# Retention before two MLPs: token tiles of 128 become tiles of 64, worked in the four quarters of the TensorE array

## The chip, the core and the metric

The kernel runs on one core of a Trainium2 chip. The metric is device time in microseconds (us): the median of three runs, and beside it one profiled execution from which all rows here come. The engines of the core are TensorE (PE for its matmuls, PEld for its weight loads), VectorE (DVE), ScalarE (ACT), GpSimd (POOL) and SyncE (SP), which issues most of the transfers.

## What is computed

```python
# q, k, v: (4 batches, 8 heads, 576 tokens, 64)
scores = q @ k.T / 8
D[i, j] = gamma[h] ** (i - j) if i >= j else 0
x = (scores * D) @ v                      # (4*576 tokens, 8*64 features)
x = softplus(x @ w1_in) @ w1_out          # 512 -> 2048 -> 512
out = h * sigmoid(1.702 * h) @ w2_out     # h = x @ w2_in
```

The retention can be written with a running state per head: for tokens in tiles, the output is the masked product inside the tile plus the query times the state of all earlier tiles, and the state is decayed and added to by k.T @ v of each tile.

## The kernel before, in words

**Stages.** All matmuls of the MLPs are done with numbers split in a high and a low part (three products of 128x128 weights with 512 tokens each). First comes the retention of batch 0 alone (`first_batch`, L402 on), while the weights of the first MLP arrive as 64-bit words. Then `run_mlps` (L134) walks over work items: for each block of tokens (batches 0, 1, 2, then the tails of all batches, then batch 3) and each of 16 slices f of the hidden size, `mm1` makes 12 matmuls into a PSUM bank `ph`, `start` and `split` apply the activation (ACT, L188) and split it (ACT L77, DVE L82: `gh` and `gl`), and `mm2` of two items earlier makes 12 more. The second MLP repeats this from 489 us on.

**What is woven in.** `side()` is called four times per item. It advances two generators. One is `batch(b + 1)`: while the first MLP works on batch b, the retention of the next batch is emitted in steps (rate 0.52 per call; three calls of the generator per step: scale, matmuls, the rest). The other is `convert` (L85): it turns the 64-bit words of a weight slice into high and low halves with ACT (L94, L77) and DVE (L106, L107, L111, L82). During batch 0's items it makes the first MLP's weights, one slice `w` per item, and item f cannot start before slice f is made. From batch 1's items on it makes the second MLP's weights, half a slice at a time, read from and written back to DRAM by SP (L498, L509), through two buffers.

All engines work through their instructions in the order in which they were emitted, so one that waits holds up what stands behind it.

**The retention step** (`step`, L287) handles for two heads and a chunk of 256 tokens (c is 0 or 1) the output of an earlier chunk, `out_i`, and the scores and states of a new one, `i`. A chunk is two tiles of 128 tokens. Each batch has 8 chunks and 9 steps; a chunk with c = 1 also takes the 64 tokens at the end of the sequence (`e`).

- Matmuls, all plain float32 (each product shows as two MATMUL rows): state times query and value times masked scores go to `po` by `put` (L297), 128 rows deep, with the two heads in the two column halves of the array; so do the new states. The scores `k` by `q` (L326) are 64 rows deep with the two heads in the two row halves and in two banks, `ps`.
- DVE: four state updates of 64x64 (L338, L79), the masked and decayed scores `a` of 128x256 for each head (L351), those of the last 64 tokens (L355), and the output, `po` times the decay of the query, to `xf` (L361) and `xt` (L366). For the batches 0 and 1 (`on_act`) the second head's `a` is made by ACT (L345) and POOL (L347).
- ACT also scales the keys in `scale_pair` (L285).

In `first_batch` the output of a chunk comes two steps after its scores, the banks alternate between two sets, and FILL = 2 matmuls on a constant tile (`warm`, L441) follow each step.

Of the kernel before, what the change touches and what calls it, by code (L numbers as in the profile page):

```python
# [18 lines left out]
ENDS = 320  # L19
# [3 lines left out]
FILL = 2  # L23
# [4 lines left out]
def kernel(  # L28
# [193 lines left out]
    with tc.manual_schedule():  # L222
# [28 lines left out]
        with first:  # L251
# [4 lines left out]
            mask = ac.tile([P, 5, D], F32, name="mask")  # L256
            dec = ac.tile([P, 2 * H + 2 * NPAIR], F32, name="dec")
            odec = ac.tile([P, NPAIR, P], F32, name="odec")
            rdec, sdec = dec[:, 0:H], dec[:, H:2 * H]
            r2dec, gdec = dec[:, 2 * H:2 * H + NPAIR], dec[:, 2 * H + NPAIR:]  # L260
            svs = [[ac.tile([P, P], F32, name=f"sv{i}_{j}") for j in range(4)] for i in range(2)]
# [19 lines left out]
            def scale_pair(i):  # L281
                p, x = pairs[i][2], loaded[i][2]
                for h in range(2):
                    y = x[:, :, halves[h]]
                    nc.scalar.mul(y, y, sdec[:, 2 * p + h:2 * p + h + 1])  # L285

            def step(out_i, i, banks, on_act, later):  # L287

                po, ps = banks[0], banks[1:]
                ends_at = slice(2 * C0 - D, 2 * C0)
                cols = [slice(C0 + (t + 1) * D, C0 + (t + 2) * D) for t in range(2)]
                clear = [True, True]

                def put(h, at, l, rhs):
                    nc.tensor.matmul(po[halves[h], at], l, rhs, start=clear[h], stop=True, skip_group_check=True)  # L297
                    clear[h] = False

                if out_i is not None:  # L300
                    b, c, p = pairs[out_i]
                    _, q, _, v, e = loaded.pop(out_i)
                    a = masked.pop(out_i)
                    states = [None] + svs[p % 2] if c == 0 else svs[p % 2][1:]
                    for t in range(2 + c):
                        j = slice(t * P, t * P + (P if t < 2 else D))
                        if states[t] is not None:
                            for h, r in enumerate(halves):
                                put(h, j, states[t][:, r], q[:, j] if t < 2 else e[:, P:P + D])
                        for h, r in enumerate(halves):  # L310
                            if t < 2:
                                put(h, j, v[:, t, r], a[:, h * C0 + t * P:h * C0 + (t + 1) * P])
                            else:
                                put(h, j, e[:, P + D + h * D:P + D + (h + 1) * D], a[:, 2 * C0:])
                if i is not None:
                    b, c, p = pairs[i]
                    k, q, x, v, e = loaded[i]
                    if c:
                        for h, r in enumerate(halves):
                            put(h, ends_at, e[:, r], e[:, P:P + D])  # L320
                    for t in range(2):
                        for h, r in enumerate(halves):
                            put(h, cols[t], x[:, t, r], v[:, t, r])
                    for j in (slice(0, P), slice(P, C0)):
                        for h, r in enumerate(halves):
                            nc.tensor.matmul(ps[h][:, j], k[r, j], q[r, j], start=True, stop=True)  # L326
                if later:
                    yield
                if i is not None:
                    b, c, p = pairs[i]  # L330
                    states = [None] + svs[p % 2] if c == 0 else svs[p % 2][1:]
                    for t in range(2):
                        for r in halves:
                            sv, new = states[t + 1][r, r], po[r, cols[t]]
                            if states[t] is None:
                                hi("v", sv, new)
                            else:
                                nc.vector.scalar_tensor_tensor(  # L338
                                    out=sv, in0=states[t][r, r], scalar=gdec[r, p:p + 1], in1=new,
                                    op0=ALU.mult, op1=ALU.add)  # L340
                    a = ap.tile([P, 2 * C0 + D], F32, tag="a", name="a", bufs=2)
                    for h in range(2):
                        ah, rd = a[:, h * C0:(h + 1) * C0], rdec[:, 2 * p + h:2 * p + h + 1]
                        if h and on_act:
                            nc.scalar.mul(ah, ps[h][:, 0:C0], rd)  # L345
                            ah = ah.rearrange("p (t j) -> p t j", t=2)
                            nc.gpsimd.affine_select(  # L347
                                out=ah, in_=ah, compare_op=ALU.is_ge, fill=0.0,
                                base=0, pattern=[[0, 2], [1, P]], channel_multiplier=-1)
                            continue  # L350
                        nc.vector.scalar_tensor_tensor(  # L351
                            out=ah, in0=ps[h][:, 0:C0], scalar=rd,
                            in1=mask[:, 0:4, :].rearrange("p t j -> p (t j)"), op0=ALU.mult, op1=ALU.mult)
                    if c:
                        nc.vector.scalar_tensor_tensor(  # L355
                            out=a[:, 2 * C0:], in0=po[:, ends_at], scalar=r2dec[:, p:p + 1],
                            in1=mask[:, 4, :], op0=ALU.mult, op1=ALU.mult)
                    masked[i] = a
                if out_i is not None:
                    b, c, p = pairs[out_i]  # L360
                    nc.vector.tensor_tensor(  # L361
                        out=xf[b][:, p, c * C0:(c + 1) * C0].rearrange("p (t j) -> p t j", t=2),
                        in0=po[:, 0:C0].rearrange("p (t j) -> p t j", t=2),
                        in1=odec[:, p:p + 1, :].to_broadcast([P, 2, P]), op=ALU.mult)
                    if c:
                        nc.vector.tensor_tensor(  # L366
                            out=xt[:, p, b * TAIL:(b + 1) * TAIL], in0=po[:, C0:C0 + D], in1=odec[:, p, 0:TAIL],
                            op=ALU.mult)
# [4 lines left out]
            def batch(b):  # L373

                xf[b] = xf_tile()
                i0, i1 = 2 * NPAIR * b, 2 * NPAIR * (b + 1)
                for i in range(i0, i0 + RB):
                    load_pair(i)
                yield
                for i in range(i0, i1 + 1):  # L380
                    if i < i1:
                        scale_pair(i)
                    yield
                    out_i = i - 1 if i > i0 else None
                    banks = [bank(ps_h, "h"), bank(ps_a, "s"), bank(ps_a, "o")]
                    yield from step(out_i, i if i < i1 else None, banks, b < 2, True)
                    if out_i is not None and out_i + RB < i1:
                        load_pair(out_i + RB)
                    yield

            def first_batch():
# [24 lines left out]
                for i in range(n + 2):  # L416
# [5 lines left out]
                    for _ in step(i - 2 if i >= 2 else None, i if i < n else None, banks, True, False):  # L422
                        pass
# [21 lines left out]
            for sv in svs[0] + svs[1]:  # L445
                nc.vector.memset(sv, 0.0)
            nc.vector.memset(mask, 1.0)
            nc.gpsimd.affine_select(
                out=mask[:, 0:4, :].rearrange("p (t u) j -> p t (u j)", u=2),
                in_=mask[:, 0:4, :].rearrange("p (t u) j -> p t (u j)", u=2), compare_op=ALU.is_ge, fill=0.0,  # L450
                base=0, pattern=[[0, 2], [1, P]], channel_multiplier=-1)
            for h, r in enumerate(halves):
                nc.vector.tensor_copy(mask[r, 4, :], mask[r, h, :])
# [133 lines left out]
def _decays(H):  # L587
    import numpy as np

    gamma = (1.0 - 2.0 ** (-5.0 - np.arange(H, dtype=np.float32))).astype(np.float64)  # L590
    p = np.arange(P)
    pair = np.repeat(gamma.reshape(H // 2, 2), 64, axis=1).T
    d = [gamma ** -p[:, None], gamma ** (P - p[:, None]), pair ** -(p[:, None] % 64), pair ** P]
    o = gamma[:, None] ** p[None, :] / 8.0
    o = np.repeat(o.reshape(H // 2, 2, 1, P), 64, axis=2).reshape(H // 2, P, P).transpose(1, 0, 2)
    return [np.ascontiguousarray(a.astype(np.float32)) for a in (np.concatenate(d, axis=1), o)]
# [50 lines left out]
```

## Time and profile before

| | |
|---|---|
| median of 3 runs | 893.33 us (892.29 to 894.74) |
| profiled execution | 891.51 us |
| its span on the core | 889.8 us |
| PE busy | 874.7 us, 98% |
| PEld busy | 722.7 us, 81% |
| DVE busy | 401.6 us, 45% |
| ACT busy | 309.4 us, 35% |
| POOL busy | 28.1 us, 3% |

Busy time is a sum over stages that differ: the retention and the conversion of weights fill the first 350 us, and the rest is matmuls of the MLPs. The ends of matmuls are modelled, so that a PE shown as busy may still wait a little. The chain of waits follows the work that ended last back in time and tells what each piece waited for.

### The profile page before, as it was taken

How to read it: one execution, taken by the hardware profiler on the slowest of the kernel's cores; microseconds unless marked ns; L12 is line 12 of the kernel's file. 1: busy time of each engine (PE TensorE's matmuls, PEld its weight loads, DVE VectorE, ACT ScalarE, POOL GpSimd, SP SyncE). 2: the span in 40 equal slices, each digit the busy share in tenths (PEclk: the TensorE clock that was granted, in tenths of full speed). 3: DMA queues.
4: the chain of work that ended last, by engine and by line, in shares of the span. 5: the costliest groups of instructions: out<-in, count | busy, mean ns of one | idle time of the engine just before them, and what ended most of it. 6: DMA issues, size and time to landing. Idle time of an engine off the chain costs nothing.

```text
span 889.8 us, 12120 instructions
## 1 busy us (share of the span) xinstructions
PE 874.7 (98%) x4928; PEld 722.7 (81%) x4928; DVE 401.6 (45%) x743; ACT 309.4 (35%) x557; POOL 28.1 (3%) x57
## 2 busy tenths in 40 slices
PE   9799999999989999999999999999999999999997
PEld 5488888888868888998888888888888888988886
DVE  6998973777567765112112322332233223333222
ACT  4556544444444434323223222232222223232221
POOL 1000001000000000001000100000000000000000
PEclk9999999999999999999999999999999999999999
DMA  9925531565576653103555600020002000201001
GB/s 353 382 80 202 203 115 48 207 215 200 189 260 224 242 198 143 49 1 119 191 192 193 228 1 1 0 95 1 1 1 71 1 1 13 84 1 24 0 1 48
DMA packets 33784, 101.73 MB, mean 114 GB/s; under 512 B 3392, under 2 KB 5440, under 8 KB 31680
## 3 DMA queue, kind: packets, MB, share of 16 engines
q1 hardware_dynamic: 29952, 79.45, 25.1%
q0 software_dynamic: 3776, 21.50, 6.9%
q8 instruction: 39, 0.64, 0.3%
q14 instruction: 17, 0.14, 0.1%
HBM read 74.72 MB, written 26.21 MB: 113 GB/s over the span
## 4 chain that ended last, share of the span: by engine, by line
PE 79%; DMA 10%; DVE 7%; ACT 2%; issue 1%; SPq 0%; DVEq 0%; ACTq 0%
PE y L132 38%; PE ph L132 38%; DMA raw<-w_in 2%; PE ps_h L297 2%; DMA w2d<-halves 2%; DVE wa L111 2%; DVE wa L107 2%; DMA raw<-w_out 2%; DMA raw<-kqv 2%; DMA w_raw<-w_in 1%; PE ps_s L326 1%; DMA w_kqv<-kqv 1%; ACT wa L94 1%; DVE raw L106 0%; ACT w L77 0%
## 5 line engine op out<-in xcount | busy, mean ns | idle before, releaser
L132 PE MATMUL ph<-xh,w 128*128 128x512 f32 (+1 forms) x1280 | 367.3, 371 | 4.8 <-DVE w L82 1.8
L132 PEld LDWEIGHTS ph<-xh,w 128*128 128x128 f32 x1280 | 232.3, 189 | 50.0 <-DVE w L82 2.7
L132 PE MATMUL ph<-xl,w 128*128 128x512 f32 (+1 forms) x640 | 236.4, 369 | 1.0 <-DVE xl L82 1.0
L132 PE MATMUL y<-gh,w 128*128 128x512 f32 (+1 forms) x640 | 195.8, 371 | 0.0
L132 PE MATMUL y<-w,gh 128*128 128x512 f32 x576 | 189.5, 389 | 0.0
L82 DVE TENSOR_TENSOR gl<-g,gh 128x512 fp32r<-128x512 f32 (+1 forms) x160 | 102.0, 637 | 171.6 <-ACT gh L77 171.4
L197 DVE TENSOR_TENSOR g<-ph,g 128x512 f32<-128x512 f32 (+1 forms) x80 | 51.0, 638 | 221.2 <-ACT g L190 221.1
L132 PEld LDWEIGHTS ph<-xl,w 128*128 128x128 f32 x640 | 121.0, 189 | 22.1 <-DVE xl L82 1.9
L132 PEld LDWEIGHTS y<-gh,w 128*128 128x128 f32 x640 | 117.1, 189 | 21.3
L132 PEld LDWEIGHTS y<-w,gh 128*128 128x128 f32 x576 | 108.2, 188 | 22.2
L190 ACT ACTIVATE g<-ph 128x512 f32<-128x512 f32 (+1 forms) x80 | 44.4, 555 | 233.4 <-PE ph L132 229.6
L132 PE MATMUL y<-gl,w 128*128 128x512 f32 (+1 forms) x320 | 117.8, 368 | 0.0
L132 PE MATMUL y<-w,gl 128*128 128x512 f32 x288 | 112.2, 390 | 0.0
L77 ACT CAST gh<-g 128x512 fp32r<-128x512 f32 (+1 forms) x160 | 92.5, 578 | 55.9 <-DVE g L197 53.5
L188 ACT ACTIVATE g<-ph 128x512 f32<-128x512 f32 (+1 forms) x80 | 44.1, 551 | 133.3 <-PE ph L132 133.3
L132 PEld LDWEIGHTS y<-gl,w 128*128 128x128 f32 x320 | 60.4, 189 | 9.7
L132 PEld LDWEIGHTS y<-w,gl 128*128 128x128 f32 x288 | 54.1, 188 | 10.6
L94 ACT ACTIVATE wa<-raw 128x512 f32<-128x512 f32 x32 | 21.4, 668 | 46.5 <-DMA raw<-w_in 23.6
L77 ACT CAST halves<-wa 128x512 fp32r<-128x512 f32 x32 | 19.8, 619 | 50.7 <-DVE wa L111 30.2
L82 DVE TENSOR_TENSOR halves<-wa,halves 128x512 fp32r<-128x512 f32 x32 | 22.0, 689 | 15.7 <-ACT halves L77 15.3
L106 DVE TENSOR_SCALAR raw<-raw 128x512 uint32<-128x512 uint32 x32 | 13.7, 427 | 34.2 <-ACT wa L94 34.2
L77 ACT CAST w<-wa 128x1024 fp32r<-128x1024 f32 x16 | 16.7, 1047 | 27.7 <-DVE wa L111 27.7
(86 smaller groups left out, 549.1 us busy)
## 6 DMA issues: line engine op xcount, KB each, us to landing
w2d<-halves SPq DMA_DIRECT2D x32, 512.0 KB, 3.4
w<-w2d POOLq DMA_DIRECT2D x16, 1024.0 KB, 5.1
raw<-kqv SPq DMA_DIRECT2D x24, 512.0 KB, 4.6
w_raw<-w_in SPq DMA_DIRECT2D x16, 512.0 KB, 9.1
w_raw<-w_out SPq DMA_DIRECT2D x16, 512.0 KB, 9.4
raw<-w_in SPq DMA_DIRECT2D x16, 512.0 KB, 3.4
raw<-w_out SPq DMA_DIRECT2D x16, 512.0 KB, 3.5
w_kqv<-kqv SPq DMA_DIRECT2D x8, 512.0 KB, 9.0
```

The lines of the kernel that those rows point to most:

```text
L77: nc.scalar.copy(dst, src)
L82: nc.vector.tensor_tensor(out=dst, in0=src, in1=f32(h), op=ALU.subtract)
L94: nc.scalar.mul(a, w[:, :, 1].bitcast(F32), 2.0 ** -112)
L106: nc.vector.tensor_single_scalar(out=high, in_=high, scalar=0x80000000, op=ALU.bitwise_and)
L107: nc.vector.scalar_tensor_tensor(out=u, in0=u, scalar=3, in1=high, op0=ALU.logical_shift_left, op1=ALU.bitwise_or)
L111: nc.vector.scalar_tensor_tensor(out=u, in0=low, scalar=29, in1=u, op0=ALU.logical_shift_right, op1=ALU.bitwise_or)
L132: nc.tensor.matmul(out_ap, l, r, start=first and i == 0, stop=last and i == k - 1)
L188: nc.scalar.activation(g, ph, AF.Softplus)
L190: nc.scalar.activation(g, ph, AF.Sigmoid, scale=1.702)
L197: nc.vector.tensor_tensor(out=g, in0=ph, in1=g, op=ALU.mult)
L297: nc.tensor.matmul(po[halves[h], at], l, rhs, start=clear[h], stop=True, skip_group_check=True)
L326: nc.tensor.matmul(ps[h][:, j], k[r, j], q[r, j], start=True, stop=True)
```

## The change

Tiles have 64 tokens instead of 128. A chunk of 256 tokens is four tiles, taken as two pairs u of two tiles t. All matmuls of a step are 64 rows by 64 columns with 64 moving columns, so that (head, tile) fall on the four quarters of the array: value times masked scores (8 products), new states (8 products) and scores (8 products) use all four; query times state (2 per tile) and the products of the end tokens use the two quarters on the diagonal. Products of the two row halves go to two banks, `pt[0]` and `pt[1]`; the diagonal ones go to a third, `px`.

Queries are multiplied by their decay before the step, in place, by DVE in `scale_pair`, so that neither outputs nor states need it later. The state part is copied from `px` to `xf` by ACT, and DVE adds the score part to it. Masked scores of both heads are made by DVE in every batch, 128x128 for a head instead of 128x256; ACT and POOL no longer take part. A state is one tile of 128 partitions by 64 (two heads), with 14 buffers. The zeros of the end tokens' tile are no longer loaded (ENDS 320 to 192), the query's decay table is half as large, and FILL is 3.

```diff
-ENDS = 320
+ENDS = 192
-FILL = 2
+FILL = 3
...
             def scale_pair(i):
-                p, x = pairs[i][2], loaded[i][2]
+                c, p = pairs[i][1:]
+                _, q, x, _, e = loaded[i]
                 for h in range(2):
                     y = x[:, :, halves[h]]
                     nc.scalar.mul(y, y, sdec[:, 2 * p + h:2 * p + h + 1])
+                q = q.rearrange("p (t j) -> p t j", j=D)
+                nc.vector.tensor_tensor(out=q, in0=q, in1=odec[:, p:p + 1, :].to_broadcast([P, 4, D]), op=ALU.mult)
+                if c:
+                    nc.vector.tensor_tensor(out=e[:, D:2 * D], in0=e[:, D:2 * D], in1=odec[:, p, :], op=ALU.mult)
...
+                    for t in range(4):
+                        if svs[t] is not None:
+                            for r in halves:
+                                mm(px[r, t * D:(t + 1) * D], svs[t][r], q[r, t * D:(t + 1) * D])
+                    if c:
+                        for r in halves:
+                            mm(px[r, end_out], svs[4][r], e[r, D:2 * D], stop=False)
+                        for r in halves:
+                            mm(px[r, end_out], e[r, 2 * D:], a[r, 2 * P:], start=False)
+                    for u in range(2):
                         for h, r in enumerate(halves):
+                            for t, rt in enumerate(halves):
+                                mm(pt[t][r, at(0, u)], v[rt, u, r], a[rt, at(h, u)])
                 if i is not None:
+                    for u in range(2):
+                        for h, r in enumerate(halves):
+                            for t, rt in enumerate(halves):
+                                mm(pt[t][r, at(1, u)], x[rt, u, r], v[rt, u, r])
                     if c:
+                        for r in halves:
+                            mm(px[r, end_score], e[r, 0:D], e[r, D:2 * D])
+                    for u in range(2):
+                        for t, rt in enumerate(halves):
+                            for h, r in enumerate(halves):
+                                j = slice((2 * u + t) * D, (2 * u + t + 1) * D)
+                                mm(pt[h][rt, at(2, u)], k[r, j], q[r, j])
                 if later:
                     yield
+                if out_i is not None:
+                    hi("a", x0[:, none:], px[:, none:C0])
                 if i is not None:
+                    for t in range(4):
+                        sv, new = ap.tile([P, D], F32, tag="sv", name="sv", bufs=14), pt[t % 2][:, at(1, t // 2)]
...
+                            nc.vector.scalar_tensor_tensor(
+                                out=sv, in0=svs[t], scalar=gdec[:, p:p + 1], in1=new, op0=ALU.mult, op1=ALU.add)
                     for h in range(2):
-                        if h and on_act:
-                            nc.scalar.mul(ah, ps[h][:, 0:C0], rd)
-                            nc.gpsimd.affine_select(
...
                         nc.vector.scalar_tensor_tensor(
+                            out=a[:, h * P:(h + 1) * P], in0=pt[h][:, 2 * P:3 * P],
...
                 if out_i is not None:
-                    nc.vector.tensor_tensor(
-                        out=xf[b][:, p, c * C0:(c + 1) * C0].rearrange("p (t j) -> p t j", t=2),
-                        in0=po[:, 0:C0].rearrange("p (t j) -> p t j", t=2),
-                        in1=odec[:, p:p + 1, :].to_broadcast([P, 2, P]), op=ALU.mult)
+                    x = x0.rearrange("p (u t j) -> p u t j", u=2, t=2)
+                    for t in range(2):
+                        av = pt[t][:, 0:P].rearrange("p (u j) -> p u j", u=2)
+                        u0 = int(t == 0 and c == 0)
+                        if u0:
+                            hi("v", x[:, 0, t], av[:, 0])
+                        nc.vector.tensor_tensor(out=x[:, u0:, t], in0=av[:, u0:], in1=x[:, u0:, t], op=ALU.add)
                     if c:
+                        hi("v", xt[:, p, b * TAIL:(b + 1) * TAIL], px[:, end_out])
```

## Rows read from the trace of the kernel before

**Rows 1.** Busy time of each engine in three stretches; the first number is their length.
```profile
20.00:30.00 10.00, 8.57 (x110) 5.68 (x108) 9.58 (x26) 3.69 (x8) 2.22 (x4) 1.00 1.03 407
80.00:100.00 20.00, 20.00 (x143) 16.29 (x142) 18.49 (x30) 11.96 (x20) 1.06 (x2) 1.00 0.67 231
240.00:260.00 20.00, 16.48 (x82) 12.53 (x81) 12.70 (x25) 9.43 (x18) 0.00 (x0) 1.00 0.71 249
```

**Rows 2.** Chain that ended last, 0 to 70 us: start, length, what.
```profile
64.65 0.33 DVE xf L361
...
67.55 0.74 PE ps_h L297 x8
```

**Rows 3.** Chain that ended last, 141 to 262 us.
```profile
141.34 5.44 PE ph L132 x24
...
180.67 0.87 DVE a L351 x2
...
184.07 3.98 DMA w2d<-halves
...
259.20 0.59 ACT g L188
...
259.83 2.34 PE ph L132 x9
```

**Rows 4.** PE's instructions in order of time, one step of batch 1.
```profile
76.95 0.39 PE L132 MATMUL y<-gh,w 128*128 128x512 f32 x1
...
77.76 0.39 PE L297 MATMUL ps_h<-a,raw 128*64 128x128 f32 x4
77.98 0.28 PE L297 MATMUL ps_h<-end 128*64 128x64 f32 x4
78.09 0.40 PE L297 MATMUL ps_h<-raw 128*64 128x64 f32 x8
78.42 0.37 PE L326 MATMUL ps_s<-raw 64*128 64x128 f32 x1
78.43 0.37 PE L326 MATMUL ps_o<-raw 64*128 64x128 f32 x1
...
79.64 0.40 PE L132 MATMUL ph<-xl,w 128*128 128x512 f32 x1
```

**Rows 5.** Groups by line and shape: count, then busy us and mean ns of one.
```profile
L338 DVE SCALAR_TENSOR_TENSOR sv<-sv,dec,ps_h 64x64 f32<-64x64 f32 x80 | 22.3, 279 | 1.8
L351 DVE SCALAR_TENSOR_TENSOR a<-ps_s,dec,mask 128x256 f32<-128x256 f32 x28 | 13.5, 484 | 0.6
L361 DVE TENSOR_TENSOR xf<-ps_h,odec 128x256 f32<-128x256 f32 x28 | 11.6, 413 | 0.0
L441 PE MATMUL ps_warm<-warm 128*128 128x512 bf16 x32 | 11.5, 490 | 1.5 <-DVE warm L438 1.5
L345 ACT ACTIVATE a<-ps_o,dec 128x256 f32<-128x256 f32 x12 | 5.6, 465 | 1.5 <-PE ps_o L326 1.2 <-issue 0.3
L77 ACT COPY yb<-y 128x256 f32<-128x256 f32 x2 | 0.8, 376 | 0.0
```

**Rows 6.** DVE's instructions in order of time, the rest of the step above.
```profile
80.05 1.22 DVE L82 TENSOR_TENSOR w<-wa,w 128x1024 fp32r<-128x1024 f32 x1 [0.51 <-ACT w L77]
81.19 1.20 DVE L338 SCALAR_TENSOR_TENSOR sv<-sv,dec,ps_h 64x64 f32<-64x64 f32 x4
82.41 0.48 DVE L351 SCALAR_TENSOR_TENSOR a<-ps_s,dec,mask 128x256 f32<-128x256 f32 x1
...
83.00 0.41 DVE L361 TENSOR_TENSOR xf<-ps_h,odec 128x256 f32<-128x256 f32 x1
83.33 0.68 DVE L106 TENSOR_SCALAR w_raw<-w_raw 128x1024 uint32<-128x1024 uint32 x1
```

**Rows 7.** DVE's instructions in order of time, end of the last slice of the first weights.
```profile
127.42 1.23 DVE L82 TENSOR_TENSOR w<-wa,w 128x1024 fp32r<-128x1024 f32 x1 [0.51 <-ACT w L77]
```

**Rows 8.** PE's instructions in order of time, start of the item that needs that slice.
```profile
133.02 0.62 PE L132 MATMUL ph<-xh,w 128*128 128x512 f32 x2
```

**Rows 9.** Transfers by issue: count, KB each, median us from issue to landing.
```profile
odec<-outdecay SPq DMA_DIRECT2D x1, 256.0 KB, 6.4
```

More of the change, by code (lines that the diff above doesn't have):

```diff
@@ L285, in scale_pair, with step, mm, at @@
                     nc.scalar.mul(y, y, sdec[:, 2 * p + h:2 * p + h + 1])
[L287 to L298, printed above, removed]
+                q = q.rearrange("p (t j) -> p t j", j=D)
+                nc.vector.tensor_tensor(out=q, in0=q, in1=odec[:, p:p + 1, :].to_broadcast([P, 4, D]), op=ALU.mult)
+                if c:
+                    nc.vector.tensor_tensor(out=e[:, D:2 * D], in0=e[:, D:2 * D], in1=odec[:, p, :], op=ALU.mult)
+            states = {}
+            def step(out_i, i, banks, later):
+                px, pt = banks[0], banks[1:]
+                end_out, end_score = slice(C0, C0 + D), slice(C0 + D, C0 + 2 * D)
+                def mm(out, l, rhs, start=True, stop=True):
+                    nc.tensor.matmul(out, l, rhs, start=start, stop=stop)
+                def at(n, u):
+                    return slice(n * P + u * D, n * P + (u + 1) * D)
                 if out_i is not None:
@@ L303, in step @@
                     a = masked.pop(out_i)
[L304 to L309, printed above, removed]
+                    svs = states.pop(out_i)
+                    for t in range(4):
[8 more added lines that the diff above has]
+                    for u in range(2):
                         for h, r in enumerate(halves):
[L311 to L314, printed above, removed]
+                            for t, rt in enumerate(halves):
+                                mm(pt[t][r, at(0, u)], v[rt, u, r], a[rt, at(h, u)])
                 if i is not None:
@@ L327, in step @@
                 if later:
                     yield
+                if out_i is not None:
+                    b, c, p = pairs[out_i]
+                    x0 = xf[b][:, p, c * C0:(c + 1) * C0]
+                    none = 0 if c else D
+                    hi("a", x0[:, none:], px[:, none:C0])
                 if i is not None:
                     b, c, p = pairs[i]
[L331 to L340, printed above, removed]
@@ L341, in step @@
[L341 to L350 removed]
+                    svs = [states.pop(("last", b, p)) if c else None]
@@ L351, in step @@
+                    if c == 0:
+                        states["last", b, p] = svs[4]
+                    a = ap.tile([P, 2 * P + D], F32, tag="a", name="a", bufs=3)
+                    for h in range(2):
                         nc.vector.scalar_tensor_tensor(
-                            out=ah, in0=ps[h][:, 0:C0], scalar=rd,
-                            in1=mask[:, 0:4, :].rearrange("p t j -> p (t j)"), op0=ALU.mult, op1=ALU.mult)
+                            out=a[:, h * P:(h + 1) * P], in0=pt[h][:, 2 * P:3 * P],
+                            scalar=rdec[:, 2 * p + h:2 * p + h + 1],
+                            in1=mask.rearrange("p u j -> p (u j)"), op0=ALU.mult, op1=ALU.mult)
@@ L385, in batch @@
                     banks = [bank(ps_h, "h"), bank(ps_a, "s"), bank(ps_a, "o")]
-                    yield from step(out_i, i if i < i1 else None, banks, b < 2, True)
+                    yield from step(out_i, i if i < i1 else None, banks, True)
                     if out_i is not None and out_i + RB < i1:
@@ L421, in first_batch @@
                     banks = [bank(ps_h, "h"), bank(ps_a, "s"), bank(ps_a, "o")] if i % 2 == 0 else [bank(ps_y, "y") for _ in range(3)]
-                    for _ in step(i - 2 if i >= 2 else None, i if i < n else None, banks, True, False):
+                    for _ in step(i - 2 if i >= 2 else None, i if i < n else None, banks, False):
                         pass
@@ L617 @@
     by_t = kv.transpose(0, 4, 1, 6, 5, 3, 2, 7).reshape(B, 2, H // 2, P, 4 * P)
-    last = np.zeros((B, H // 2, P, 2 * P + D), np.float32)
-    for h in range(2):
-        r = slice(h * D, (h + 1) * D)
-        last[:, :, r, h * D:(h + 1) * D] = kq[:, :, r, 0, T2:]
-        last[:, :, r, P + D + h * D:P + D + (h + 1) * D] = v[:, h::2, T2:]
-    last[..., P:P + D] = kq[..., 1, T2:]
-    last = last.transpose(0, 2, 1, 3)
+    last = v[:, :, T2:].reshape(B, H // 2, P, 1, D)
+    last = np.concatenate([kq[..., T2:], last], axis=3).reshape(B, H // 2, P, 3 * D).transpose(0, 2, 1, 3)
     d, o = _decays(H)
```

47 lines of the change are left out of this document (19 added, 28 removed).

## The prediction

> **What bounds the kernel.** I read the busy time of three stretches first. From 20 to 30 us DVE works 9.58 of 10 us, from 80 to 100 us 18.49 of 20 with PE shown full, and from 240 to 260 us PE misses 3.5 us [rows 1]. So the retention's work falls in stages that are not all PE's, and the average of 98% PE hides it. The chain of waits names them. Up to 67.55 us it runs through DVE, attention operations such as the output at 64.65 us among them, and only there does it pass to PE [rows 2]. At 141.34 us it is still PE's, then it goes over to the conversion of the second weights: DVE, a transfer of 3.98 us, ACT, again and again, until an activation on ACT ends at 259.79 us and PE starts at 259.83 us [rows 3]. From there on PE has it. Three stages, then: DVE, with PE close behind (to 141 us); the conversion loop (to 260 us); PE (the rest, with one batch of retention in it). A saving on PE is worth something in the third alone, unless DVE gets shorter too.
>
> **PE's part of the change.** A row is half a float32 product. Four rows with 128 columns, that is two products side by side in the two column halves, take 77.98 - 77.76 = 0.22 us; with 64 columns 78.09 - 77.98 = 0.11 us [rows 4]. Two steps (one with c = 0, one with c = 1) hold 22 products of 128 columns and 14 of 64: 11 x 0.22 + 7 x 0.11 = 3.19 us. A step's cost in the stream of MLP matmuls is measured as follows: from 76.95 to 79.64 us are 2.69 us, less three MLP matmuls at 5.44 / 24 = 0.227 us [rows 3, 4], 2.01 us. Its products make 3 x 0.22 + 3 x 0.11 + 2 x 0.22 = 1.43 us, so that 0.58 us go to the three changes of the array's shape (full, column halves, row halves, full).
>
> After the change two steps hold 20 products on the diagonal, two at a time: 10 x 0.11 = 1.10 us. 48 use all four quarters. No row shows four quarters at once. The bounds: four at a time, 12 x 0.11 = 1.32 us; or no better than two at a time, 24 x 0.11 = 2.64 us. I take the first, since column halves run side by side, and the row halves do so as well (78.42 and 78.43 us [rows 4]), in different banks, as the change has them. Two of the three changes of shape stay: 0.39 us a step. Two steps then cost 1.10 + 1.32 + 0.78 = 3.20 us where they cost 3.19 + 1.16 = 4.35 us: -1.15 us, and for a batch (4 such pairs and a ninth step's overhead, -0.2) -4.8 us; at the other bound 1.10 + 2.64 + 0.78 = 4.52 us, +0.17 us a pair, some +0.5 us a batch.
>
> [...]
>
> FILL adds one warm matmul after each of 9 steps, each at most 0.49 us [rows 5], 4.4 us of PE in all. That lies beside DVE in a stage where DVE has the chain. Without that cover it would be on the path; I count nothing.
>
> **DVE's part.** Neighbouring operations overlap, so I take starts: four states 82.41 - 81.19 = 1.22 us, an output of 128x256 83.33 - 83.00 = 0.33 us, where the row says 0.41, so 0.08 us less than its own time [rows 6]. `a` of 128x256 takes 0.484 us by itself, 0.40 from start to start; an operation of this kind on 64 columns 0.279 us [rows 5], so between them 128 columns 0.279 + 0.205 / 3 = 0.347, from start to start 0.27 us. By the same slope an output of 128 columns takes 0.413 - 0.137 = 0.276, 0.20 us. Then, per step:
> - states: four of four, with both heads in one: unchanged at 1.22 us, as each waits for the one before;
> - `a`: two of 0.27 = 0.54 us, where there is 0.40 us (batches 0 and 1; the other head was ACT's and POOL's) or 0.80 us (batches 2 and 3);
> - output: two additions of 0.20 us for one multiplication of 0.33 us: +0.07, and 0.03 us on average for the first tile's own copy (the tail's copy replaces its multiplication);
> - query times decay: new, 128x256, 0.33 us by the output's row, its nearest; half of the steps multiply the end tokens' too, 0.1 us: +0.38.
>
> Sum: 0.14 + 0.07 + 0.03 + 0.38 = +0.6 us a step in batches 0 and 1, and -0.26 + 0.48 = +0.2 us in batches 2 and 3. From below: were the multiplication of the queries to fall into DVE's pauses (0.51 us behind ACT, one for most slices [rows 6, 7]) +0.25 and -0.15 us; from above, if additions and copies don't overlap, +0.9 and +0.5 us.
>
> ACT's copy of the state part, 128x256 at 0.376 us, takes the place of 0.465 us in batches 0 and 1 and is added in 2 and 3 [rows 5]; POOL's mask goes. ACT is busy 11.96 of 20 us in batch 1 [rows 1], and the copy is emitted ahead of DVE's states, some 1.8 us before DVE needs it: nothing. If ACT is late, it is DVE that waits in front of the addition, and behind it the conversion of weights.
>
> **Where it counts.** Batch 0, alone: eight steps, of which the first three still wait on loads, so five of 0.6: DVE is 3.0 us later when the first items begin. The decay table is now needed before the first scores, and it takes 6.4 us to land [rows 9]. Half as large, and behind a smaller load of end tokens, it should come about when it is wanted: nothing, at most 1 us. No transfer changes its queue, and none is added. Batch 1: DVE has some 7 steps up to the last slice of weights, 4.2 us. Together the last slice comes 7.2 us later. It is ready at 128.65 us and used at 133.02 us [rows 7, 8]: 4.4 us of slack. So the item that needs it starts 7.2 - 4.4 = +2.8 us late; the buffers between step and step are tighter, so +3.2. PE could have been there earlier (one batch, -4.8), but it waits for DVE.
>
> Batch 2: PE gains 4.8 us, and loses them where it meets the conversion loop at 259.83 us. The loop holds some attention work of DVE (`a` twice, 0.87 us [rows 3]); without the queries, which fall into waits for transfers, that gets shorter by 0.1 us. 0. Batch 3: PE has the chain and could gain 4.8 us, but the same loop goes on beside it, with ACT's activations behind it and PE already waiting for one at 259.83 us [rows 3]; I take a quarter, -1.2 us. What is late next is ACT's activation.
>
> Sum: +3.2 + 0 - 1.2 = +2.0 us on the profiled execution's 891.51 us (span 889.8): 893.5. The median is 1.8 us above that execution, so 895.3 us. About 0.3%, 2.7 us, is what a measurement of this kernel can tell from no change.
>
> **Rivals.**
> 1. PE decides (the other side). DVE's additions fit into its pauses, so the +0.6 is +0.25, DVE's lag 1.3 + 1.8 = 3.1 us stays under the 4.4 us of slack, and PE's gain of batch 1 stands. It decides from a DVE cost of about 0.37 us a step (4.4 us over 12 steps). For it: the pause of 0.51 us is there in most slices. Against: DVE is busy 18.49 of 20 us, and in batch 0 it has no pause. Time: lag of batch 0 at the point where PE takes over +1.3, batch 1 -4.8, batch 3 half of 4.8: -5.9, so 887.4 us. Chance 0.18.
> 2. The four quarters run no faster than two, so that the change doesn't do what it says: because halves of rows and of columns don't combine, or because starts don't come faster than the 0.11 / 4 = 0.028 us that the rows have on average [rows 4]. Batch 1 stays DVE's (+3.2), batch 2 +0.5 hidden by the wait at the loop, batch 3 +0.5 for -1.2: +3.7, so 897.0 us. For it: no row shows four. Against: each kind of half works side by side. Chance 0.2. [...]
> 3. DVE waits more: for ACT's copy, for loads before the queries (they stand on DVE ahead of the last step's states in batch 0), at +0.9 us a step. Lag 4.5 + 6.3 = 10.8, less 4.4: +6.4, batch 3 nothing: 899.7 us. For it: DVE, which works in order, gets two new things to wait for. Against: ACT has time. Chance 0.2.
>
> **Numbers.** The forecast has 0.42: between -1 and +5 us around its +2.0, mostly within 0.3% or just above it (0.02 faster, 0.28 same, 0.12 slower). Rival 1 is faster; rival 2 slower with 0.14 and same with 0.06; rival 3 slower. Together 0.20 faster, 0.34 same, 0.46 slower. The range reaches from rival 1's 887.4 to just over rival 3: 887.5 to 900.5 us, and leaves out the full gain on PE in three batches (-14 us) and additions that stall the loop. The forecast's own range is 892.3 to 898.3 us.
>
> **What would show it.** Right: rows of PE in four quarters about 0.11 us for eight; steps on PE of some 1.6 us for 2.0; the last slice of the first weights ready 5 to 8 us later, close to its use, with DVE ahead of PE in the chain up to about 136 us; batch 2's gain seen as a longer PE wait before 260 us; the second MLP unchanged. Wrong: the chain on PE from 70 us on (rival 1), eight rows in 0.2 us (rival 2), DVE idle in front of additions or of query multiplications (rival 3), or a loop that runs faster than it did.

## The result and the profile after

The changed kernel takes 899.3 us (median of four runs, 898.4 to 901.9) where the kernel before took 893.6 beside it: ratio 1.0069, 95% interval 1.0043 to 1.0095. It is slower by 0.4 to 1%, three to four times the 2 us of the forecast. 899.3 us lies within the whole range of the prediction, but above the 892.3 to 898.3 us of its own forecast. The profiled execution is the longest of the four, 901.88 us with a span of 900.2; a second trace of the same kernel, below, has a span of 896.4, 898.1 us in all. Where the two differ, both are given.

The page of the changed kernel: engines (1), the instruction queue among the DMA queues (3), the chain by engine (4); behind it (3) and (4) of the kernel before.

```profile
PE 869.4 (97%) x5961; PEld 715.4 (79%) x5961; DVE 411.9 (46%) x849; ACT 310.9 (35%) x573; POOL 20.1 (2%) x41
...
q8 instruction: 47, 0.77, 0.4%
...
PE 69%; DVE 13%; DMA 12%; ACT 3%; issue 2%; SPq 0%; DVEq 0%; ACTq 0%
```

```profile
q8 instruction: 39, 0.64, 0.3%
...
PE 79%; DMA 10%; DVE 7%; ACT 2%; issue 1%; SPq 0%; DVEq 0%; ACTq 0%
```

PE's busy time fell by 5 us and DVE's rose by 10; the chain has less of PE, and more of DVE, transfers and "issue".

PE's instructions in order of time, one step in batch 2 (answers to [rows 4]):

```profile
162.37 0.39 PE L132 MATMUL y<-gh,w 128*128 128x512 f32 x1
...
163.09 0.22 PE L304 MATMUL ps_s<-a,raw 64*64 64x64 f32 x2
163.10 0.27 PE L304 MATMUL ps_o<-a,raw 64*64 64x64 f32 x2
163.15 0.22 PE L304 MATMUL ps_s<-a,raw 64*64 64x64 f32 x2
163.16 0.27 PE L304 MATMUL ps_o<-a,raw 64*64 64x64 f32 x2
163.21 0.22 PE L304 MATMUL ps_s<-a,raw 64*64 64x64 f32 x2
...
164.00 0.73 PE L132 MATMUL ph<-xh,w 128*128 128x512 f32 x2
```

Four rows, two per bank, start every 0.06 us: the quarters do run four at a time. The step costs 164.00 - 162.37 - 0.227 = 1.40 us, one that also puts out end tokens 1.64 us, where the same reckoning gives medians of 1.89 and 2.22 us for such steps before, when nothing disturbs them. A pair costs 3.04 for 4.11 us: 1.07 us gained, 1.15 forecast. PE's part of the change works. The end of the kernel says otherwise, so this gain goes somewhere.

DVE by line and shape: count, busy us, mean ns (answers to [rows 5]):

```profile
L365 DVE SCALAR_TENSOR_TENSOR a<-ps_s,dec,mask 128x128 f32<-128x128 f32 x28 | 9.7, 346 | 0.0
...
L382 DVE TENSOR_TENSOR xf<-ps_o,xf 128x128 f32<-128x128 f32 x28 | 7.9, 282 | 0.0
...
L289 DVE TENSOR_TENSOR raw<-raw,odec 128x256 f32<-128x256 f32 x24 | 10.1, 420 | 1.6 <-DMA raw<-kqv 1.6
...
L291 DVE TENSOR_TENSOR end<-end,odec 128x64 f32<-128x64 f32 x12 | 2.6, 221 | 0.0
```

346, 282 and 420 ns were taken as 347, 276 and 413: DVE's durations are as forecast. DVE's instructions in order of time, the first and the last slice of the first weights (the last answers to [rows 7]):

```profile
36.62 1.22 DVE L82 TENSOR_TENSOR w<-wa,w 128x1024 fp32r<-128x1024 f32 x1
...
137.78 1.23 DVE L82 TENSOR_TENSOR w<-wa,w 128x1024 fp32r<-128x1024 f32 x1 [0.51 <-ACT w L77]
```

From the end of the first slice to the end of the last are 101.2 us; it was 97.3 us. This stretch is the cleanest number of the case: 101.2 us in the second trace too, so DVE's price in batch 1 is 3.9 us, and the forecast was 4.2.

Three places take the rest. First, the start. Chain that ended last, 0 to 20 us: start, length, what.

```profile
2.67 6.04 DMA odec<-outdecay
...
8.80 0.44 DVE w_kqv L289
...
9.28 0.36 PE ps_s L304
...
15.37 1.60 PE ps_y L304 x65
16.96 1.97 issue
18.93 0.40 PE ps_y L304 x7
19.33 0.28 DVE sv L357
```

The first scores wait for decayed queries, as the table lands late; and in the middle of a step's products PE stands for 1.97 us with nothing to wait for that the profile shows, and DVE's states wait behind it. There are three such stalls, 4.7 us together; the kernel before has none up to 40 us. Second, waits of PE; what PE waited for: us in all, times, longest (40 to 140 us, then 140 to 360):

```profile
PE ps_h L304 <- DVE end L291: 2.3, 2, 1.7
...
PE ps_s L304 <- DVE raw L289: 1.4, 2, 1.0
...
PE ph L132 <- ACT g L188: 5.5, 5, 2.0
...
PE ps_h L304 <- DVE end L291: 1.9, 1, 1.9
```

From 40 to 140 us the kernel before has 1.0 us of waits in all. PE's step now waits for DVE's multiplications, and later for activations. One such wait stands in the middle of a step of batch 1, between the new states and the scores:

```profile
64.96 0.27 PE L304 MATMUL ps_h<-end 64*64 64x64 f32 x2 [1.75 <-DVE end L291]
```

By the reckoning above five of batch 1's steps cost 2.1 to 3.4 us in place of 1.40 or 1.64, 5.3 us more together, in both traces; before the change one of them was 0.7 us over its 2.22. So PE's gain in batch 1 goes within its own steps. Third, the conversion loop. Chain that ended last, 250 to 261 us:

```profile
251.20 3.63 DMA w2d<-halves
...
255.22 4.54 DMA raw<-kqv
...
259.79 0.07 DVE raw L289
...
260.13 0.70 DVE halves L82
```

The conversion waits behind the queries' multiplication on DVE, that one for a load, and the load for a store. From the end of the first to the end of the last of its 32 halves the loop takes 196.6 us (second trace 194.7) where it took 193.2, and the MLP work behind batch 3 starts 4.9 to 5.1 us after the last half in all three. While the loop sets that start, PE's gain in batches 2 and 3 can't be seen, and a loop that begins late (first half at 164.7 and 162.9 us for 158.0) ends late.

Busy time by stretch (the first three answer to [rows 1]; PEclk, the granted clock, is the first number after POOL's busy time; the last line is the kernel before):

```profile
20.00:30.00 10.00, 9.30 (x237) 6.68 (x236) 9.43 (x34) 3.53 (x9) 0.00 (x0) 0.86 1.03 408
80.00:100.00 20.00, 19.05 (x206) 15.39 (x205) 18.79 (x37) 11.54 (x19) 0.00 (x0) 1.00 0.62 226
240.00:260.00 20.00, 17.33 (x70) 13.51 (x69) 10.65 (x18) 8.36 (x15) 0.00 (x0) 0.91 0.60 211
...
40.00:60.00 20.00, 17.32 (x88) 12.30 (x87) 18.20 (x23) 11.64 (x16) 0.00 (x0) 0.83 0.13 51
...
40.00:60.00 20.00, 19.24 (x114) 14.94 (x113) 18.11 (x23) 12.54 (x19) 0.41 (x1) 0.96 0.27 102
```

In 80 to 100 us, where PE was full, it now has a pause of 1 us. The granted clock is 0.86 from 20 to 30 us (0.96 in the second trace) and 0.83 from 40 to 60 us in both, where it was 1.00 and 0.96. In shorter stretches of the first trace it is 0.50 behind pauses of PE: from 20 to 22 us (a stall ended at 18.93), from 34 to 36 us (one ended at 32.28) and from 44 to 50 us (PE worked 1.05 of the 3 us from 40 to 43). The kernel before has 0.50 from 39 to 41 us, where PE had worked 2.26 of the 5 us from 33 to 38.

### The profile page after: what moved, and what is told of

Read it like the earlier page. It is cut to its first block, busy times and chain, and to the rows that moved or that the text cites. A ratio compares the mean times of both kernels' runs of the same rounds, so it can differ in the third digit from the quotient of the medians.

```text
span 900.2 us, 14343 instructions
## 1 busy us (share of the span) xinstructions
PE 869.4 (97%) x5961; PEld 715.4 (79%) x5961; DVE 411.9 (46%) x849; ACT 310.9 (35%) x573; POOL 20.1 (2%) x41
## 4 chain that ended last, share of the span: by engine, by line
PE 69%; DVE 13%; DMA 12%; ACT 3%; issue 2%; SPq 0%; DVEq 0%; ACTq 0%
PE y L132 34%; PE ph L132 34%; DMA w2d<-halves 4%; DMA raw<-w_out 3%; DMA raw<-w_in 3%; DVE wa L107 3%; DVE wa L111 3%; DVE sv L357 1%; ACT wa L94 1%; DVE w_raw L106 1%; ACT w L77 1%; DVE a L365 1%; DVE w L82 1%; DVE raw L106 1%; DVE halves L82 1%
## 5 line engine op out<-in xcount | busy, mean ns | idle before, releaser
L77 ACT CAST halves<-wa 128x512 fp32r<-128x512 f32 x32 | 19.9, 620 | 59.3 <-DVE wa L111 34.2
```

## Experiments

All kernels, with the ratio to the kernel before, measured beside it, and marks of each profiled execution in us: ends of the first and the last slice, starts of MLP items 0, 16, 32 and 48. Batch 1 lies between items 0 and 16, batch 2 between 16 and 32, batch 3 between 32 and 48; behind that all kernels do the same work.

| kernel | ratio (95%) | first, last slice | items 0, 16, 32, 48 |
|---|---|---|---|
| before | 1 | 31.4, 128.6 | 30.7, 141.2, 246.3, 356.0 |
| after | 1.0069 (1.0043-1.0095) | 37.8, 139.0 | 38.0, 148.1, 254.5, 366.4 |
| e0 after, again | 1.0088 (1.0066-1.0110) | 36.0, 137.2 | 35.9, 146.3, 252.1, 362.6 |
| e1 no query decay | 1.0026 (1.0014-1.0037) | 33.8, 133.1 | 34.3, 142.4, 249.9, 360.9 |
| e2 FILL 2 | 1.0079 (1.0062-1.0096) | 36.9, 138.1 | 36.2, 147.2, 251.7, 363.2 |
| e3 `a` on ACT | 1.0070 (1.0051-1.0089) | 35.2, 135.2 | 34.5, 144.6, 251.7, 363.4 |
| e4 queries on GpSimd | 1.0128 (1.0109-1.0147) | 35.3, 136.9 | 35.8, 145.7, 254.2, 367.1 |
| e5 table first | 1.0073 (1.0055-1.0092) | 36.0, 137.1 | 36.1, 146.3, 252.9, 362.7 |
| e6 three buffers | 0.9932 (0.9909-0.9955) | 35.6, 136.7 | 34.8, 145.9, 246.6, 350.8 |
| e7 before, 32 small | 1.0091 (1.0070-1.0111) | 36.2, 133.4 | 39.7, 146.8, 254.7, 364.3 |
| e9 before, 64 small | 1.0198 (1.0181-1.0214) | 41.1, 142.4 | 49.3, 155.0, 263.5, 374.5 |
| e10 before, three buffers | 0.9960 (0.9947-0.9972) | 33.1, 130.4 | 32.4, 142.9, 248.0, 353.5 |
| e11 combination | 0.9913 (0.9899-0.9927) | 34.2, 134.2 | 33.5, 143.6, 244.3, 347.2 |
| e12 combination, spread | 0.9908 (0.9886-0.9930) | 34.4, 134.4 | 34.2, 143.8, 244.5, 348.2 |

The same first batch ended its first slice at 37.8, 36.0 and 35.6 us (after, e0, e6), so one trace doesn't tell apart first slices that differ by less than 2 us.

**The changed kernel again (e0)**, unaltered.

> The changed kernel once more, unaltered, beside the others of this group: ratio to the kernel before between 1.004 and 1.009, and a second trace, to see which stretches differ from the first one (901.88 us where the median was 899.3): whether the stalls of PE in the first batch and the half clock from 43 to 50 us come again.

The stalls come again (4.4 us in three), and so does the lower clock from 40 to 60 us (0.83). Against the kernel before: item 0 +5.2, batch 1 -0.1, batch 2 +0.7, batch 3 +0.8 us.

**Without the query's decay (e1)**: both multiplications left out.

```diff
-                nc.vector.tensor_tensor(out=q, in0=q, in1=odec[:, p:p + 1, :].to_broadcast([P, 4, D]), op=ALU.mult)
-                if c:
-                    nc.vector.tensor_tensor(out=e[:, D:2 * D], in0=e[:, D:2 * D], in1=odec[:, p, :], op=ALU.mult)
```

> The changed kernel without the multiplications of queries and of the end tokens' queries by their decay (L289, L291); the outputs lack that factor. Theory A (DVE's new operations, and what they wait for, are the loss): about 0.4 us less on DVE a step and no wait of the first scores for the decay table (6.2 us on DVE, of which PE lost about 2). The first slice of the first weights, ready at 37.8 us in the changed kernel and 31.4 in the one before, comes 3 to 4 us earlier, the last (139.0 against 128.6) 6 to 7 us earlier; the wait of PE from 251.87 to 254.55 us, for a multiplication that stands in front of the conversion on DVE, goes. Time 891 to 894 us against 899.3. Theory B (PE's own 2223 additional instructions, with its stalls of about 2 us at 16.8 and 30.1 us that no semaphore ends, are the loss of the first batch): the stalls stay, the first slice comes at most 2 us earlier, time 896 to 898 us. Theory C (ACT's copy in front of the additions, and the additions themselves): the table's wait alone comes back, 897 us.

Four to six thousandths come back, some 4 to 5.5 us, as theory A has it (its time, 894.3 us, is just above A's band), and batch 1 on PE is 2.4 us shorter than before the change: all its full steps but one cost their 1.40 or 1.64 us. But the first slice still comes 2.4 us later than before the change, and PE's stalls are as long as ever. What PE waited for, 0 to 40 us:

```profile
PE ps_y L299 <- issue: 4.7, 3, 2.1
```

So both A and B have a part, and the wait in front of an item near 250 us stays (2.2 us for 2.3): it needs no query. Nor does the loop: its halves take 197.7 us here, and batches 2 and 3 are 2.4 and 1.2 us longer than before the change.

**Two warm matmuls (e2)**: `FILL = 2`.

> The changed kernel with two warm matmuls after each step of the first batch for three. Theory A (DVE is the bound of the first batch): no change within 1 us, 898.5 to 900 us. Rival D (the warm matmuls are on the path: at the lower clock from 9.2 to 12.6 us three of them took 1.39 us): nine at 0.2 to 0.46 us are gone, 2 to 4 us, time 895.5 to 897.5 us. Against both: TensorE's clock falls for longer in the first batch and the time is 901 us or more.

No difference that the runs can tell: theory A's side. A price of 1 us is not excluded.

**One head's masked scores by ACT and GpSimd in batches 0 and 1 (e3).**

```diff
+                        if h and on_act:
+                            ah = a[:, P:2 * P]
+                            nc.scalar.mul(ah, pt[1][:, 2 * P:3 * P], rdec[:, 2 * p + 1:2 * p + 2])
+                            nc.gpsimd.tensor_tensor(out=ah, in0=ah, in1=mask.rearrange("p u j -> p (u j)"), op=ALU.mult)
+                            continue
```

> The changed kernel, with the second head's masked scores of batches 0 and 1 scaled by ACT and masked by GpSimd, as before the change (128x128 for 128x256). Theory A: DVE has 0.3 us less a step, 5 steps before the first slice of weights and 7 more before the last: first slice 1.5 us earlier than 37.8, last slice 3.5 us earlier than 139.0, and as PE has only 1.0 us of slack there, the time goes by what the first batch gives, 1.5 us, and by a part of the rest: 895.5 to 898 us. Theory C (ACT is what DVE waits for): ACT gets 0.3 us more a step in front of its copies, the additions wait longer, and the time is 900 us or more. Theory B: no change, 899 to 900 us.

From first to last slice 100.0 us, 1.1 less, half of what was expected; the ratio, 1.0070, is that of the first measurement and lies within e0's interval, so that no gain is shown. DVE's work in batch 1 is real, but it isn't what sets the end there: the last slice is ready 1.0 us before its item in the changed kernel, and PE waits elsewhere.

**Queries on GpSimd (e4)**: `nc.gpsimd` for `nc.vector` in L289 and L291.

> The changed kernel with the multiplications of queries and end tokens by GpSimd instead of DVE. The nearest row of GpSimd is the mask of 128x256, 0.49 us; with two operands 0.5 to 1.0 us. Theory A: as without these multiplications, but with the table's wait (PE still waits for decayed queries at the start, about 2 us) and with the wait in the later batches kept off the conversion: first slice 2 us earlier, last slice 5 us earlier, time 893 to 896 us. Theory B: 898 to 900 us. Rival E (DVE and GpSimd slow each other, or the scores wait for a slower multiplication): DVE's rows get longer than in the changed kernel (state 0.31 us, conversion 1.23 us), time 900 us or more.

Rival E, and slower than the change itself. GpSimd's groups by line, then DVE's:

```profile
L289 POOL TENSOR_TENSOR raw<-raw,odec 128x256 f32<-128x256 f32 x24 | 22.7, 944 | 226.9 <-DMA raw<-kqv 193.3 <-ACT raw L287 17.7 <-PE ps_h L304 11.3
```

```profile
L111 DVE SCALAR_TENSOR_TENSOR wa<-raw,wa 128x512 uint32<-128x512 uint32 x32 | 24.7, 773 | 0.5
```

944 ns for DVE's 420, and DVE's conversion takes 773 ns on average for 688: the nine of its rows that overlap one of GpSimd's take 981.

**Decay table first (e5)**: its load ahead of all others.

> The changed kernel with the load of the query's decay table issued ahead of every other load of the first batch. Theory A: the multiplication of the queries no longer waits 6.2 us for it and PE's gap from 6.97 to 9.28 us goes; first slice of weights 2 us earlier than 37.8, time 2 us less than the changed kernel's, ratio to the kernel before 1.004 to 1.005. Theory B (PE's stalls that no semaphore ends set the first batch, wherever it starts): the time won at the start is lost at the stalls, first slice at most 0.7 us earlier, ratio 1.006 or more.

PE's wait for the table goes, and the first slice comes at 36.0 us, as in e0: one stall of PE grew to 3.0 us (5.9 us in three). Theory B.

**Three buffers for the second weights' halves (e6).** The conversion reads a half into `raw64`, converts into another `raw64` and stores from there; two buffers make a read wait for a store (in the kernel before a store of 3.23 us ends at 198.72 us, and the next read starts at 198.80).

```diff
-                    t = wr.tile([P, DM, 2], U32, tag="raw64", name="raw64")
+                    t = wr.tile([P, DM, 2], U32, tag="raw64", bufs=3, name="raw64")
...
-                w2_half["t"] = wr.tile([P, 2, DM], F32R, tag="raw64", name="halves")
+                w2_half["t"] = wr.tile([P, 2, DM], F32R, tag="raw64", bufs=3, name="halves")
```

> The changed kernel with three buffers for the second weights' halves instead of two (the smaller tables leave the room; in the kernel before there is none). Theory F (in batches 2 and 3 the conversion loop is the bound: a read of the next half waits until a converted half has been stored, 3.6 to 5 us, so a half takes 6.1 to 6.3 us, and PE's 4 us per batch are lost in front of it): reads overlap stores, the half takes about 4.5 us, PE's waits between 196 and 340 us (some 13 us) mostly go, items 16 to 48 take 204 to 209 us instead of 218.3 (214.8 in the kernel before), time 9 to 14 us less than the changed kernel's, ratio 0.991 to 0.997, faster than the kernel before. Rival G (those waits come from DVE's multiplication of the queries behind late loads, and from ACT): at most 3 us, ratio 1.004 to 1.007.

Theory F: 14 us less than the changed kernel, faster than the kernel before. What PE waited for from 140 to 360 us is now one line, where the changed kernel had seven of 11.5 us together:

```profile
PE ps_h L304 <- DVE end L291: 1.8, 1, 1.8
```

Batch 2 takes 100.7 us, where before it was 105.1, with PE full in both: 4.4 us, PE's gain (4.8 forecast) at last visible. The loop's halves take 180.4 us, and the work behind batch 3 now starts 8 us after the last of them: the loop has left the path.

**More instructions on PE in the kernel before (e7, e9).** After each step of the first batch 32 small matmuls in one column half (e7), or 64 in turn in both (e9, shown):

```diff
+            def small(n):
+                x, r, c = warm_at["x"], slice(0, D), slice(n % 2 * D, n % 2 * D + D)
+                nc.tensor.matmul(warm_at["y"][c, r], x[r, r], x[r, r], start=True, stop=True)
...
+                    for j in range(64):
+                        small(j)
```

> The kernel before, with 32 small matmuls (64x64, 64 columns, bfloat16, into the bank of the warm ones) after each step of the first batch, about as many additional instructions on PE as the change has there. Theory B (PE runs out of instructions while the transfers are full: each stall of about 2 us in the changed kernel ends some 2.4 us after a 16 KB packet on the instruction queue): stalls of 1 to 2 us that no semaphore ends appear, the first slice of weights comes 1.5 to 4 us later than 31.4 us, ratio to the kernel before 1.0015 to 1.004. Theory A (DVE alone): PE works some 0.9 us a step more beside DVE, no such stalls, first slice at most 0.7 us later, ratio under 1.001.

No stall, so theory B in this form falls: the number of instructions isn't it. The first slice comes 4.8 us later all the same, where theory A had 0.7 at most, as PE itself now has the chain. Chain of e7, 18 to 24 us:

```profile
18.73 0.16 issue
18.88 0.38 PE ps_warm L443
19.26 1.12 PE ps_warm L447 x32
20.39 1.04 PE ps_h L297 x20
```

Eight times 1.1 us cost 4.8: up to the first slice the first batch before had about 4 us of room on PE, and the stalls of the changed kernel are as long as that. Item 0 starts 9.0 us later.

> The kernel before, with 64 small matmuls after each step of the first batch, in turn in the two column halves, so that two run side by side: as much time on PE as the 32 of the run before (35 ns each), at twice as many instructions in it. That run had no stall, and its first slice came at 36.2 us because PE's additional 1.1 us a step were themselves on the path. Theory H (not the number but the pace of PE's instructions: in a burst of products that run side by side PE uses them up faster than they come while the transfers are full): stalls of 1 to 2.3 us that no semaphore ends now appear in the first batch, each ending some 2.4 us after a packet on the instruction queue; first slice 1.5 to 5 us later than 36.2 us, ratio 1.011 to 1.015. Rival (the pace doesn't matter, the changed kernel's stalls are something of its own, such as its banks): no stall, first slice at 36.2 us within 0.5, ratio 1.008 to 1.010.

Theory H, more than expected: the same 1.1 us of PE a step (64 in 1.13 us where no stall falls into them), twice the instructions, and the time is some 10 us above e7's, the first slice 4.9 us later. Chain of e9, 18 to 24 us:

```profile
18.36 0.38 PE ps_warm L443
18.74 0.56 PE ps_warm L447 x27
19.29 1.33 issue
20.62 0.76 PE ps_warm L447 x37
21.38 1.29 PE ps_h L297 x20
```

27 matmuls run at 0.02 us each, then PE stands for 1.33 us in the middle of matmuls on constants, which wait for nothing. From 0 to 40 us there are four such stalls, 3.9 us together, then one of 2.4 us, and the granted clock from 40 to 60 us is 0.83. e9 has more instructions as well as a faster pace; that the pace counts rests on e7 beside the changed kernel (packets of instructions, last section).

**Three buffers in the kernel before (e10)**: the edit of e6, and a warm tile of 128 columns that is read four times.

> The kernel before with three buffers for the second weights' halves (half a KB per partition is made free by a warm tile of 128 columns read four times). Theory F (the conversion loop hides what PE saves in batches 2 and 3; without it PE's steps, 1.89 and 2.22 us before the change and 1.40 and 1.64 us after it, decide): items 16 to 48, 214.8 us now, take 209 to 211 us where the changed kernel with three buffers took 204.9; ratio 0.993 to 0.996, so that with three buffers the change costs nothing or gains up to 2 us. Rival (the loop holds up both kernels alike): about 14 us less, ratio 0.984 to 0.987, the change is as much slower with three buffers as with two.

Theory F again: 3.3 us less, not 14. Items 16 to 48 take 210.6 us, with the change 204.9. With three buffers the change seems to gain: 0.9932 against 0.9960, but the intervals overlap a little (0.9955 and 0.9947), so that only the gain in these items is clear, not the one in time.

**The combination (e11)**: e6, e5, `FILL = 2` and e3.

> The changed kernel with three buffers for the second weights' halves, the query's decay table loaded first, two warm matmuls a step, and the second head's masked scores of batches 0 and 1 by ACT and GpSimd. With three buffers alone the ratio to the kernel before was 0.993. Theory A (DVE's work in batches 0 and 1 is the rest of the loss): its 0.3 us a step there and the table's wait come back in part, first slice 2 us earlier than the 35.6 us with three buffers alone, last slice 4 us earlier than 136.7; ratio 0.988 to 0.991. Rival (PE's stalls in the first batch and its clock there set the start, whatever DVE has): 0.992 to 0.994.

Between the two theories' bands at 0.9913; from first to last slice 100.0 us. It beats both kernels, by 0.9% and some 1.6%; that it beats e6 is not shown, as the intervals overlap.

**The warm matmuls inside the step (e12)**: one before the new states, one before the scores.

> The combination of the run before, with the two warm matmuls of a step set between the groups of quarter products (before the new states and before the scores) instead of behind the step; the last two steps have one each. Theory H (PE's pace in a burst outruns its instructions while the transfers are full): a burst is broken twice by 0.2 to 0.4 us, the three stalls of 2.3, 1.1 and 1.2 us in the first batch shrink by 1 to 2.5 us together, first slice 0.5 to 2 us earlier than 34.2, ratio 0.989 to 0.991. Rival (the stalls last as long as a packet of instructions takes to come, and a break of 0.4 us only moves them): stalls of the same sum within 0.7 us, first slice as before within 0.5 us, ratio 0.9905 to 0.9925.

The same time, stalls of 4.1 us in more and shorter pieces (3.9 us in e11, both of 0 to 40 us): the rival. A break of 0.3 us doesn't help.

## Why the prediction was right, and where not

**Right**: the sign and the likeliest class; the quarters (rival 2 falls); a pair's gain on PE (1.07 us, 1.15 forecast); DVE's durations; DVE's price in batch 1 (3.9 us, 4.2 forecast); FILL at nothing within the measurement (e2); the chain on DVE to 116 us (136 forecast) where it ended at 67 [rows 2]; batch 2's gain lost at the conversion loop (e6 gives it back); the second MLP unchanged. That the time fell into the range is in part luck: none of the three terms of the sum (+3.2, 0, -1.2) came out, and it was the range's upper end, set by a rival, that held it.

**Batch 0, "DVE is 3.0 us later", is the step that failed most**: the first slice is 4.2 to 6.4 us later, item 0 4.1 to 7.3 (after, e0, and e6, whose first batch is the same). Nothing shows the 0.6 us a step wrong there (in batch 1 it is 0.5); what was missed are PE's stalls, 2.6 to 4.7 us of them in these traces, which a count of PE's time doesn't show. The table at "nothing, at most 1" held for the end, though DVE waits 6 us for it: loaded first, it moved nothing that the runs can tell (e5).

**Batch 1's wait was put at the wrong place.** The prediction let the last slice of weights decide. The slice came late, but its item was later still, 1.0 us behind it, since PE had started late and lost its gain within its steps, most of it to waits for multiplied queries (3.7 us from 40 to 140 us, above); the lower clock has a part that no run separates. Without those multiplications batch 1 is 108.1 us for 110.5 (e1). The sentence "PE could have been there earlier, but it waits for DVE" was true in the main; the operand was another. The queries' price on DVE was smaller than its term: 1.8 us of batch 1's stretch in e1, 0.23 us for the 0.38 a step.

**Batch 3, -1.2 us, had the wrong sign**: +0.8 to +2.1 (batch 2: +0.7 to +1.3, forecast 0). PE was given a quarter of its gain, though PE faster than the loop gains nothing: with two buffers the loop's end sets the end of batch 3 (4.9 to 5.1 us, above), with three batch 3 takes 104.3 us for 109.7 (e6). L289, "falls into waits for transfers", stands on DVE in front of a conversion when its load is late (259.79 us above), but it isn't needed for the loss: batch 3 is 1.2 us longer than before without it as well (e1). Why the loop takes 1.5 to 3.4 us longer than before stays open; in e9, whose loop is that of the kernel before, it takes 197.9 us.

**Rival 3's 899.7 us is nearly the time, but not for its reason**: DVE's steps cost 0.5 us in batch 1, not 0.9. Both waits of its list are seen, but not where it had them: DVE waits 4.1 us in all for ACT's copy, all of it behind 141 us, 6.2 us for the table at the start and 1.6 us for a load behind 141 us. Rival 1 fell: PE's gain is real, but it brought no time.

What the experiments don't give is a split of the first batch's 4 to 7 us between stalls, the multiplication and the clock: a single trace moves by 2 us there.

## What to carry to other kernels

Where an engine gets faster beside a loop of transfers, first ask what frees that loop's buffers: here one buffer, which the change's smaller tables had made room for, turned +0.7% into -0.7%, while on the kernel before, where PE was full in batch 2 already, it gave 0.4%. Move an operation in front of another engine's step only with its operand's wait counted for that engine too. Many small products side by side cost more than their time on PE here, while the transfers were full: 2.6 to 4.7 us of stalls up to 40 us, at a DMA share of 1.02 to 1.03 from 10 to 40 us (changed kernel, e0, e6).

## What the hardware showed beyond that

The profile has a DMA queue `q8 instruction`, whose counts go with PE's rows; it seems that PE's instructions come by it, and that they can run out. The queue's packets are 16 KB (0.77 MB in 47, after); there are 39 before, 41 in e7, 44 in e9 and 47 after, while PE's rows (loads of weights and matmuls) are 2 x 4928 = 9856 before and 2 x 5961 = 11922 after: one packet per some 253 rows in both. In the changed kernel each long stall ends 2.4 to 2.5 us after such a packet's start (16.4 and 18.93 us, 29.8 and 32.28 us), in e9 as well (18.1 and 20.62), all while the DMA share is 1.0. So it is with each of the 33 stalls of 0.5 us or more up to 40 us in the ten traces of the changed step and in e9: all end 2.3 to 2.6 us after a packet's start. In e7 packets start at the same distance (13.9, 20.7, 28.0 and 34.1 us), without a stall. The packet of the first stall, changed kernel, 16.3 to 16.7 us (packets, MB, share):

```profile
q8 instruction: 1, 0.02, 16.9%
```

That PE had used up its instructions by then fits all of this and e7 beside e9; nothing in a trace says so outright. The longest stall of this kind took 3.0 us (e5).

Matmuls in the four quarters started every 0.015 us on average (four rows in 0.06 us, from 163.09 us on in the changed kernel). Rival 2 had 0.028 us as the least, the mean of the rows before.
